# Attention with projections on one core: a new start, earlier loads of the second output weight, and a hand-ordered end

## The chip, the cores and the metric

The program runs on one core of one Trainium2 chip. The metric is the time of one execution in device microseconds (us), median of several. Runs carry a state, fast or slow: a run is called slow when it is over 1.5% longer than the fastest run of the same kernel. The ratios below compare fast runs alone; the medians are those with the few slow runs in them. Single runs of one kernel differ by 1 to 4 us here (the old kernel: 295.6 to 300.5 us in fast runs), so differences under about 1.5 us (0.5%) between two kernels are not read as results on their own.

## The reference

There are two independent problems, A and B, with equal shapes. The results stand side by side in the output.

```python
B, Sq, D = 8, 64, 448;  Hq, Hkv, Sk, Dh = 16, 8, 512, 256
q = (x @ wq).reshape(B, Sq, Hq, Dh)              # wq: 448 x 4096
k, v = k_cache, v_cache                          # each used by two query heads
p = softmax(q @ k.T * Dh**-0.5)
y = (p @ v).reshape(B, Sq, Hq*Dh) @ wo           # wo: 4096 x 448
out = concatenate([A_y, B_y], axis=-1)           # all bfloat16
```

K and V of both problems are 67 MB and are read once. wq and wo are 3.67 MB each for each problem.

## The kernel before

The work is cut into 128 units (64 for A, then 64 for B): one KV head of one batch, with its two query heads of 64 rows each as 128 rows. The program is planned in Python: every engine gets a fixed list of instructions, and waits on semaphores are put in where one engine needs another's result. TensorE (PE) does, for each unit, the transpose of K (every second unit; the other units' K is transposed by the DMA on its way in), the score matmuls, the transpose of P and the P·V matmuls. In between it does the query projection (wq) and the output projection (wo).

The loop runs over iterations `it`; in each one the stages of several units are at work:

```python
for it in range(it0, NU + D1 + 3):
    issue_dmas(it)               # loads needed up to iteration it + LEAD (5)
    ... pt_op(it - 3)            # transpose P of unit it-3
    ... qproj_chunk(...)         # query projection, up to two chunks
    ... qk_op(it); max_op(it)    # scores of unit it
    ... kt_op(it + 4)            # transpose K of unit it+4
    if it < NU - 1:              # output projection, as much as the level allows
        lvl = o_level(it)
        while o_fifo:
            if o_fifo[0][0] == 1 and o_fifo[0][1] == 3 and o_fifo[0][2] < n_tail + 0:
                break            # TAIL_GROUPS = 6 groups are kept for the end
            ...
            do_o_group(it)
    else:
        ...                      # the groups kept back, two per iteration
    ... pv_op(it - 3)
```

`o_level` spreads the output projection so that the planned TensorE time is level over the iterations that are left. All loads are issued by SyncE, in one order. K has three buffers of each kind and V has four (for two units each), so a load can be issued only when the buffer's last reader is done.

wo has one buffer for both problems, so each of B's eight wo loads (448 KB each) must wait for A's last use:

```python
def dma_wo(prob, g):
    plan.add("sp", lambda e: e.dma_start(wo_sb[:, g], src),
             writes=[("wo_sb", g)], ...)
def do_o_group(it):
    last = oproj_op(prob, bp, g)
    if prob == 0:
        if o_count[(0, bp)] >= 1 and bp == 3:
            dma_wo(1, g)         # SyncE waits here for TensorE
```

One more detail matters. An instruction can carry one wait; when an operation has several, the planner puts the others on earlier instructions of the same engine, up to 24 back ("hoisting"). So the wait for the first wq load stands on the last transpose of x, which does not need wq.

## Time and profile before

| | before |
|---|---|
| time, first four runs | 297.53 us median (296.32 to 297.9) |
| span of the profiled run | 295.8 us |
| TensorE busy | 281.9 us, 95% |
| first projection matmul / first score matmul | 8.1 / 18.9 us |
| TensorE waits for DMA after 20 us | 3.8 us |

From the page of the old kernel: the span, busy time and instructions by engine, and the 40 slices of TensorE's busy share and of its granted clock (in tenths).

```profile
span 295.8 us, 7089 instructions
...
PE 281.9 (95%) x2833; PEld 193.2 (65%) x2878; DVE 194.7 (66%) x519; ACT 177.2 (60%) x458; POOL 87.8 (30%) x132
...
PE   6899999999999999999999999999997799999995
...
PEclk9799999999999999999999999999999999999999
```

TensorE's waits for DMA after 20 us (what waited and for which load, then us in total, times, longest):

```profile
PE bank L631 <- DMA V_sb<-in_B_v_cache_dram: 1.6, 3, 1.0
PE bank L501 <- DMA K_sb<-in_B_k_cache_dram: 1.4, 2, 0.7
PE bank L566 <- DMA KTD_sb<-in_B_k_cache_dram: 0.8, 1, 0.8
```

TensorE is full except at the start, in slices 31 and 32, and at the very end. The timeline of TensorE at the start (start, length, line, operation, count, and in brackets the idle time before it and what ended it) shows why the first slices are poor:

```profile
1.41 3.38 PE L379 MATMUL bank<-ident 128*128 128x128 bf16 x30 [1.41 <-POOL ident L736]
4.80 1.04 PE L395 MATMUL bank<-ident,x_sb 128*112 128x128 bf16 x15
6.54 0.26 PE L395 MATMUL bank<-ident,x_sb 128*112 128x128 bf16 x1 [0.69 <-DMA wq_sb<-in_A_wq_dram]
8.12 5.27 PE L431 MATMUL bank<-xT_sb,wq_sb 112*128 112x512 bf16 x16 [1.32 <-ACT xT_sb L418]
...
15.27 3.62 PE L431 MATMUL bank<-xT_sb,wq_sb 112*128 112x512 bf16 x16
18.95 0.38 PE L501 MATMUL bank<-KT_sb,QT_sb 128*128 128x512 bf16 x1
```

L379 are warm-up matmuls, L395 the transposes of x, L431 the query projection, L460 transposes of K, L501 the scores. Fifteen transposes run at 4.80; the sixteenth stands until 6.54 for the wq load, and the projection until 8.12 for ScalarE's eviction. Its 16 matmuls then take 5.27 us; the next 16, at 15.27, take 3.62. Busy time by stretches (start:end, length, then busy time and count of PE, PEld, DVE, ACT, POOL, then granted clock, DMA share, GB/s):

```profile
8.00:20.00 12.00, 11.71 (x63) 5.41 (x65) 2.33 (x6) 5.43 (x10) 0.00 (x0) 0.86 0.91 245
100.00:140.00 40.00, 39.40 (x418) 27.70 (x424) 30.22 (x82) 26.31 (x71) 14.19 (x21) 1.00 1.15 300
220.00:240.00 20.00, 15.82 (x164) 10.31 (x164) 11.60 (x31) 8.86 (x25) 5.22 (x8) 1.00 1.14 318
```

The clock is 0.86 in the first of these stretches, and from 220 to 240 us TensorE is busy 15.8 of 20 us. The chain of waits there (start, length, what):

```profile
216.51 0.45 PE bank L501 x2
216.96 0.36 SPq L349
...
217.36 1.96 SPq L357
...
219.36 1.86 SPq L371
...
221.27 1.22 SPq L349
...
222.53 5.95 DMA K_sb<-in_B_k_cache_dram
...
228.53 0.39 PE bank L501
```

The chain leaves TensorE for SyncE's queue (SPq): the wo load (L349), a DMA transpose of K (L357), a V load (L371), another wo load, then a K load that lands 5.95 us after its issue. I read this chain as a queue held up by the wo loads' wait for TensorE.

### The profile page before, as it was taken

How to read it: one execution, taken by the hardware profiler on the slowest of the kernel's cores; microseconds unless marked ns; L12 is line 12 of the kernel's file. 1: busy time of each engine (PE TensorE's matmuls, PEld its weight loads, DVE VectorE, ACT ScalarE, POOL GpSimd, SP SyncE). 2: the span in 40 equal slices, each digit the busy share in tenths (PEclk: the TensorE clock that was granted, in tenths of full speed). 3: DMA queues.
4: the chain of work that ended last, by engine and by line, in shares of the span. 5: the costliest groups of instructions: out<-in, count | busy, mean ns of one | idle time of the engine just before them, and what ended most of it. 6: DMA issues, size and time to landing. Idle time of an engine off the chain costs nothing.

```text
span 295.8 us, 7089 instructions
## 1 busy us (share of the span) xinstructions
PE 281.9 (95%) x2833; PEld 193.2 (65%) x2878; DVE 194.7 (66%) x519; ACT 177.2 (60%) x458; POOL 87.8 (30%) x132
## 2 busy tenths in 40 slices
PE   6899999999999999999999999999997799999995
PEld 5345665776667677676766677777765467777663
DVE  1125544777687687777666668888875577777751
ACT  2467677565666666675777776665654446555551
POOL 0002221233233233333323323434422223333310
PEclk9799999999999999999999999999999999999999
DMA  7999999999999999999999999999999999999700
GB/s 207 245 249 293 356 276 338 289 369 293 278 364 291 239 358 264 278 295 345 284 273 307 320 290 304 258 331 321 289 368 300 363 295 287 294 293 289 245 18 16
DMA packets 112321, 84.09 MB, mean 284 GB/s; under 512 B 70304, under 2 KB 87712, under 8 KB 112288
## 3 DMA queue, kind: packets, MB, share of 16 engines
q1 hardware_dynamic: 112288, 83.64, 105.7%
q8 instruction: 22, 0.36, 0.5%
q14 instruction: 11, 0.09, 0.1%
HBM read 65.93 MB, written 0.92 MB: 226 GB/s over the span
## 4 chain that ended last, share of the span: by engine, by line
PE 82%; DMA 6%; ACT 5%; DVE 3%; SPq 2%; issue 1%
PE bank L590 17%; PE bank L501 16%; PE bank L431 16%; PE bank L631 15%; PE bank L460 10%; PE bank L566 8%; ACT P_sb L529 3%; DMA V_sb<-in_B_v_cache_dram 2%; DMA K_sb<-in_B_k_cache_dram 2%; DMA wq_sb<-in_A_wq_dram 2%; ACT OT_sb L609 2%; DVE negmax L520 2%; DVE KT_sb L479 1%; SPq L357 1%; SPq L371 1%
## 5 line engine op out<-in xcount | busy, mean ns | idle before, releaser
L546 POOL TENSOR_SCALAR P_sb<-P_sb,rinv 128x512 bf16<-128x512 bf16 x126 | 87.1, 692 | 195.7 <-DVE rinv L538 195.7
L520 DVE TENSOR_REDUCE negmax<-bank 128x1 f32<-128x512 f32 x128 | 88.5, 691 | 40.6 <-PE bank L501 40.2
L609 ACT ACTIVATE OT_sb<-bank 128x256 bf16<-128x256 f32 x128 | 49.0, 383 | 87.4 <-PE bank L590 87.4
L529 ACT ACTIVATE P_sb<-bank,negmax 128x512 bf16<-128x512 f32 x128 | 87.4, 683 | 0.2 <-DVE negmax L520 0.2
L575 DVE COPY PT_sb<-bank 128x512 bf16<-128x512 bf16 x128 | 54.2, 424 | 41.7 <-PE bank L566 40.2
L590 PE MATMUL bank<-PT_sb,V_sb 128*128 128x128 bf16 x1024 | 78.1, 219 | 0.0
L590 PEld LDWEIGHTS bank<-PT_sb,V_sb 128*128 128x128 bf16 x1024 | 66.0, 98 | 17.1 <-DVE PT_sb L575 0.3
L431 PE MATMUL bank<-xT_sb,wq_sb 112*128 112x512 bf16 x256 | 66.3, 387 | 1.3 <-ACT xT_sb L418 1.3
L631 PE MATMUL bank<-wo_sb,OT_sb 128*128 128x448 bf16 x256 | 59.3, 353 | 2.2 <-DMA V_sb<-in_B_v_cache_dram 1.6
L479 DVE COPY KT_sb<-bank 128x512 bf16<-128x512 bf16 x128 | 51.9, 406 | 8.3 <-PE bank L460 8.2
L566 PE MATMUL bank<-ident,P_sb 128*128 128x128 bf16 x512 | 50.0, 219 | 0.9 <-DMA KTD_sb<-in_B_k_cache_dram 0.8
L443 ACT ACTIVATE QT_sb<-bank 128x512 bf16<-128x512 f32 x64 | 38.2, 597 | 17.7 <-PE bank L431 16.5
L460 PEld LDWEIGHTS bank<-ident,K_sb 128*128 128x128 bf16 x512 | 33.2, 98 | 17.7 <-DVE KT_sb L479 4.6
L631 PEld LDWEIGHTS bank<-wo_sb,OT_sb 128*128 128x128 bf16 x256 | 23.8, 98 | 26.1 <-DMA V_sb<-in_B_v_cache_dram 4.0
L460 PE MATMUL bank<-ident,K_sb 128*128 128x128 bf16 x512 | 39.1, 219 | 0.6
L431 PEld LDWEIGHTS bank<-xT_sb,wq_sb 112*128 112x128 bf16 x256 | 22.9, 99 | 21.7 <-issue 2.2
L501 PE MATMUL bank<-KT_sb,QT_sb 128*128 128x512 bf16 x108 | 34.1, 379 | 2.5 <-DMA K_sb<-in_B_k_cache_dram 1.4
L566 PEld LDWEIGHTS bank<-ident,P_sb 128*128 128x128 bf16 x512 | 35.1, 105 | 1.6 <-DMA KTD_sb<-in_B_k_cache_dram 1.4
L501 PE MATMUL bank<-KTD_sb,QT_sb 128*128 128x512 bf16 x103 | 32.7, 379 | 1.4
L529 ACT ACTIVATION_READ_ACCUMULATOR P_sb<-bank,negmax 128x1 f32 x128 | 25.9, 202 | 0.0
L538 DVE RECIPROCAL rinv<-rowsum 128x1 f32<-128x1 f32 x128 | 19.6, 153 | 0.4 <-ACT P_sb L529 0.4
L501 PEld LDWEIGHTS bank<-KT_sb,QT_sb 128*128 128x128 bf16 x128 | 10.9, 98 | 7.6 <-DMA K_sb<-in_B_k_cache_dram 1.8
(18 smaller groups left out, 32.3 us busy)
## 6 DMA issues: line engine op xcount, KB each, us to landing
V_sb<-in_A_v_cache_dram SPq DMA_DIRECT2D x32, 512.0 KB, 6.4
V_sb<-in_B_v_cache_dram SPq DMA_DIRECT2D x32, 512.0 KB, 5.9
K_sb<-in_A_k_cache_dram SPq DMA_DIRECT2D x32, 256.0 KB, 6.5
K_sb<-in_B_k_cache_dram SPq DMA_DIRECT2D x32, 256.0 KB, 5.9
wq_sb<-in_A_wq_dram SPq DMA_DIRECT2D x8, 448.0 KB, 7.0
wo_sb<-in_A_wo_dram SPq DMA_DIRECT2D x8, 448.0 KB, 6.8
wq_sb<-in_B_wq_dram SPq DMA_DIRECT2D x8, 448.0 KB, 7.2
wo_sb<-in_B_wo_dram SPq DMA_DIRECT2D x8, 448.0 KB, 6.2
```

The costliest lines, as they stand in the source:

```text
L431: return e.matmul(banks[bk][:, 0:512], wq_sb[:, g, dtile, c0:c0 + 128], xT_sb[:, prob, dtile, :], start=(dtile == 0), stop=(dtile == 3))
L460: return e.transpose(bank[:, c:c + 128], K_sb[:, slot, kt, dt * 128:(dt + 1) * 128], ident[:, :])
L479: plan.add("dve", lambda e: e.tensor_copy(dst, bank[:, half * 512:(half + 1) * 512]), reads=[("bank", bk)], writes=[("KT_sb", ks, half)], ...
L501: return e.matmul(bank[:, 0:512], QT_sb[:, qs, b, dt, :], kt_t[:, ks, dt, :], start=(dt == 0), stop=(dt == 1))
L520: plan.add("dve", lambda e: e.tensor_reduce(negmax[:, s:s + 1], bank[:, 0:512], axis=AX.X, op=ALU.max, negate=True), reads=[("bank", bk)], ...
L529: plan.add("act", lambda e: e.activation(P_sb[:, u % NP, :], bank[:, 0:512], ACTF.Exp, bias=negmax[:, s:s + 1], scale=1.0, accum_out=rowsu ...
L546: plan.add("pool", lambda e: e.tensor_scalar(p, p, rinv[:, s:s + 1], 1.0, op0=ALU.mult, op1=ALU.mult), reads=[("rinv", s), ("P_sb", u % NP ...
L566: return e.transpose(banks_bf[PTB][:, kt * 128:(kt + 1) * 128], src, ident[:, :])
L575: plan.add("dve", lambda e: e.tensor_copy(dst, banks_bf[PTB][:, 0:512]), reads=[("bank", PTB)], writes=[("PT_sb", u % NPT)], name="ptev%d" ...
L590: return e.matmul(banks[OTB][:, dt * 128:(dt + 1) * 128], V_sb[:, slot, bl, kt, dt * 128:(dt + 1) * 128], PT_sb[:, u % NPT, kt, :], start= ...
L609: plan.add("act", lambda e: e.activation(dst, src, ACTF.Copy), reads=[("bank", OTB)], writes=[("OT_sb", ob, g, bl)], name="otev%d" % u)
L631: return e.matmul(banks[POB][:, 0:448], OT_sb[:, ob, 2 * g + hl, dt, :], wo_sb[:, g, hl * 2 + dt, :], start=first, stop=last)
```

## The change

The change has three parts, and its stated intent is to restructure the start and the end, to load wo early, and to keep wq in a ring of buffers.

```diff
 # 1. start: transposes of x in four groups without hoisted waits, four evictions,
 #    the first projection chunk waits tile by tile
-        xT_ops(0, bks=(PQB, POB), split=True)
-        sbanks = (OTB, PTB, PQB, POB)
+        xT_start((PQB, POB, OTB, PTB))          # no_hoist=True
+        sbanks = (SBK[0], PQB, POB, OTB)
...
-                qproj_chunk(0, 0, hl, dt, bk=sbanks[ci])
+                qproj_chunk(0, 0, hl, dt, bk=sbanks[ci], split=(ci == 0))
 # 2. memory: wq in a ring of four, one x and one xT, wo for both problems
-        wq_sb = sb("wq_sb", [112, 8, 4, 512], BF)
+        wq_sb = sb("wq_sb", [112, NWQ, 4, 512], BF)       # NWQ=4
-        wo_sb = sb("wo_sb", [128, 8, 4, 448], BF)
+        wo_sb = sb("wo_sb", [128, 2, 8, 4, 448], BF)
+    WO1_ITERS=(20, 56),
+            dma_reqs.append((w_lo + (g * (w_hi - w_lo)) // 7 + LEAD, 3, g, lambda g=g: dma_wo(1, g)))
-            if prob == 0:
-                if o_count[(0, bp)] >= 1 and bp == 3:
-                    dma_wo(1, g)
 # 3. end: two groups kept back instead of six, the last units written out by hand
-    TAIL_GROUPS=6,
+    TAIL_GROUPS=2,
-            if (prob, bp) != (1, 3):
-                o_total[0] -= 1
+            o_total[0] -= 1
...
+        pt_op(L - 2)
+        exp_op(L)
... (22 more lines that order the last three units by hand)
```

## The prediction

> **What bounds the kernel.** TensorE: 281.9 of the 295.8 us span (page, part 1), 82% of the chain that ended last (part 4). From 20 to 220 us it is busy 98 to 99% (busy time by stretches), in an order fixed when the program is built. So only TensorE's idle or slow time can be won back. I count four pieces.
>
> 1. Start-up wait. The timeline shows 15 of 16 transposes of x done by 5.84 us; the 16th stands until 6.54 because the wait for the first wq load (landed 6.50) was put on it. ScalarE then evicts two halves (0.61 us each); the first projection starts at 8.12.
> 2. Slow clock. The first eight projection matmuls (8.12 to 11.5) start 0.43 us apart, later ones 0.216: 1.7 us lost. Granted clock from 8 to 20 us: 0.86, or 3.4 us at half. The Trainium skill, "TensorE: Matmul & The Clock Gate", Part 1, says that an idle window of about 3.4 us halves the clock; this trace agrees in size (TensorE busy only 1.3 us between 4.8 and 8.1).
> 3. A stall from 220 to 240 us: TensorE busy 15.8 of 20, 4.2 us lost. The chain of waits goes there from the wo load through SyncE's issue queue to K and V loads. Each B wo load waits until TensorE is through with the A group in the same buffer, and all behind it in SyncE's queue waits too. SyncE's own waiting, its slack, falls from about 24 us in 40 to 4.2 us in 30 between 199 and 229, while the eight B wo loads go out; K and V then arrive late.
> 4. Tail: from the last score matmul (283.8) to the last output projection (292.95) TensorE idles only about 0.65 us. Then 0.62 us eviction and an output DMA of about 2 us.
>
> **What the change does.**
> - Transposes of x in four groups without early waits; evictions of about 0.44 us (DVE) and 0.61 us (ACT); the first projection chunk waits tile by tile. It can start when wq lands, about 6.6 us: **-1.5 us**. TensorE is then busy about 2.5 us of the same 3.4 us window, so I think (65%) the half clock does not come: **-1.1 us** expected.
> - B's wo gets its own memory (paid for by a four-slot wq ring and single x and xT), loaded over iterations 20 to 56 (about 60 to 135 us) without waiting on TensorE. The stall goes: **-4.1 us**. Cost: 3.67 MB over about 70 us, an estimate of 50 GB/s on top of about 305; the trace held 374 GB/s for 5 us without a stall, and SyncE has over 20 us of slack in each 40. **+0.5 us**.
> - Ring, x and xT reuse: a slot's readers finish two iterations before its load: **0**.
> - Tail: groups move ahead of or into the flush; the work is the same, and I estimate 0.6 to 0.8 us idle in the new dependency chain too: **0 us**.
>
> Sum -6.2: about **291 us**, range 288.8 to 293.8. Faster by over 2%: 0.55; within 2%: 0.43; slower: 0.02.
>
> **What would show each step.** First projection at about 6.6 us with 0.216 us spacing; TensorE over 98% busy between 220 and 240, no waits for K or V; less work after the last score matmul but no less idle; 60 to 135 us still over 98% busy at about 350 GB/s.
>
> **What would make it wrong.** The half clock returning at the start (+1.7); DMA saturating at iterations 20 to 56, moving the stall forward (up to +3); start-up loads not keeping up with the earlier TensorE; the tail saving more, if my chain is too long.

## The result, and the profile after

The new kernel takes 292.78 us median (292.31 to 294.32, 11 runs; a twelfth run, 295.60 us, these figures leave out); the old one in the same rounds took 297.53 (16 runs). The ratio is 0.9852, interval 0.9826 to 0.9877. Ratios here are the mean time of one kernel's fast runs over that of the other's fast runs of the same rounds, so not quite the ratio of the medians quoted. That is inside the predicted range; the prediction had given "faster by over 2%" the larger chance, 0.55.

The page of the new kernel:

```profile
span 290.7 us, 7089 instructions
...
PE 279.3 (96%) x2833; PEld 192.8 (66%) x2878; DVE 195.2 (67%) x521; ACT 176.2 (61%) x456; POOL 87.8 (30%) x132
...
PE   7999999999999999979999999999999999999995
...
PEclk9999999999999999999999999999999999999999
```

The dip at slices 31 and 32 is gone, and there is a new one at slice 18 (124 to 131 us by the slice length). TensorE at the start, where L401 are the transposes of x, L469 the projection and L547 the scores:

```profile
4.81 1.10 PE L401 MATMUL bank<-ident,x_sb 128*112 128x128 bf16 x16
6.49 3.61 PE L469 MATMUL bank<-xT_sb,wq_sb 112*128 112x512 bf16 x16 [0.57 <-DVE xT_sb L413]
...
15.66 0.38 PE L547 MATMUL bank<-KT_sb,QT_sb 128*128 128x512 bf16 x1
```

The first projection starts at 6.49 instead of 8.12 and the 16 matmuls take 3.61 us instead of 5.27. The first score matmul comes at 15.66 instead of 18.95: 3.29 us won. Busy time by stretches:

```profile
8.00:20.00 12.00, 11.83 (x73) 5.77 (x73) 3.81 (x9) 7.13 (x14) 0.46 (x1) 1.00 1.22 292
100.00:140.00 40.00, 36.88 (x389) 25.44 (x394) 27.95 (x77) 23.90 (x65) 13.14 (x20) 1.00 1.13 315
220.00:240.00 20.00, 19.84 (x214) 14.40 (x216) 15.77 (x42) 11.55 (x33) 6.92 (x10) 1.00 1.14 308
```

From 220 to 240 us TensorE is now busy 19.84 us. But from 100 to 140 us it is busy 36.88 of 40, where the old kernel had 39.40. The chain there:

```profile
116.89 0.24 PE bank L613 x4
117.13 0.10 SPq L368
...
117.28 0.84 SPq L382
...
118.16 8.40 DMA wq_sb<-in_B_wq_dram
...
126.61 1.05 PE bank L469 x4
```

It has the same form as in the old kernel: SyncE's queue, then a load that lands late, here a wq load of B. TensorE's waits for DMA after 20 us:

```profile
PE bank L469 <- DMA wq_sb<-in_B_wq_dram: 2.0, 2, 1.8
PE bank L469 <- DMA V_sb<-in_A_v_cache_dram: 0.8, 2, 0.5
```

They sum to 2.8 us, against 3.8 in the old kernel. So of the 4.1 us that I had expected from the wo part, 1.0 came.

At the end of the kernel, the time from the last unit's score weights to the end of the span fell from 12.66 to 9.24 us, by 3.42. But in the old kernel eight output projection groups stand in this stretch and in the new one three, and TensorE's busy time in it fell by as much, from 9.29 to 5.88 us. So nothing is won there net: five groups' work has moved forward.

### The profile page after: what moved, and what is told of

Read it like the earlier page. It is cut to its first block, busy times and chain, and to the rows that moved or that the text cites. A ratio compares the mean times of both kernels' runs of the same rounds, so it can differ in the third digit from the quotient of the medians.

```text
span 290.7 us, 7089 instructions
## 1 busy us (share of the span) xinstructions
PE 279.3 (96%) x2833; PEld 192.8 (66%) x2878; DVE 195.2 (67%) x521; ACT 176.2 (61%) x456; POOL 87.8 (30%) x132
## 2 busy tenths in 40 slices
DMA packets 112321, 84.09 MB, mean 289 GB/s; under 512 B 70304, under 2 KB 87712, under 8 KB 112288
## 4 chain that ended last, share of the span: by engine, by line
PE 80%; DMA 9%; ACT 4%; DVE 4%; issue 1%; SPq 1%
PE bank L639 17%; PE bank L685 16%; PE bank L547 16%; PE bank L469 14%; PE bank L506 9%; PE bank L613 8%; DMA wq_sb<-in_B_wq_dram 6%; ACT P_sb L575 3%; DMA V_sb<-in_A_v_cache_dram 2%; DVE negmax L566 1%; ACT OT_sb L659 1%; DMA x_sb<-in_A_x_dram 1%; DVE KT_sb L525 1%; SPq L382 0%; DVE xT_sb L413 0%
## 5 line engine op out<-in xcount | busy, mean ns | idle before, releaser
L469 PE MATMUL bank<-xT_sb,wq_sb 112*128 112x512 bf16 x256 | 65.0, 379 | 3.4 <-DMA wq_sb<-in_B_wq_dram 2.0
L489 ACT ACTIVATE QT_sb<-bank 128x512 bf16<-128x512 f32 x64 | 38.2, 597 | 19.5 <-PE bank L469 18.5
L613 PE MATMUL bank<-ident,P_sb 128*128 128x128 bf16 x512 | 49.4, 219 | 0.2 <-DVE P_sb L597 0.2
L469 PEld LDWEIGHTS bank<-xT_sb,wq_sb 112*128 112x128 bf16 x256 | 22.2, 97 | 23.4 <-DMA wq_sb<-in_B_wq_dram 2.4
L547 PE MATMUL bank<-KT_sb,QT_sb 128*128 128x512 bf16 x108 | 33.8, 379 | 1.1
L547 PE MATMUL bank<-KTD_sb,QT_sb 128*128 128x512 bf16 x103 | 32.7, 379 | 1.4
L547 PEld LDWEIGHTS bank<-KT_sb,QT_sb 128*128 128x128 bf16 x128 | 10.9, 98 | 5.7 <-DMA K_sb<-in_A_k_cache_dram 0.2
```

The source lines that it names most:

```text
L469: return e.matmul(banks[bk][:, 0:512], wq_sb[:, wslot, dtile, c0:c0 + 128], xT_sb[:, 0, dtile, :], start=(dtile == 0), stop=(dtile == 3))
L547: return e.matmul(bank[:, 0:512], QT_sb[:, qs, b, dt, :], kt_t[:, ks, dt, :], start=(dt == 0), stop=(dt == 1))
L613: return e.transpose(banks_bf[bk][:, kt * 128:(kt + 1) * 128], src, ident[:, :])
```

## The experiments

The k-th load in SyncE's order is a known load of the program, and the k-th weight load of TensorE a known matmul, so each load gets an issue time, a landing time, the time when its buffer's last reader was done, and the time of its first use. "Margin" below is first use minus landing.

All experiments but e4 and e8 start from the new kernel. Waits are TensorE's waits for DMA after 20 us, from the view of waits; slightly incomplete traces (2833 matmuls beside 2878 weight loads) make them good to some tenths.

| run | what | median us | ratio to old | waits, us |
|---|---|---|---|---|
| old | | 297.5 | 1 | 3.8 |
| new | | 292.8 | 0.9852 | 2.8 |
| e1 | wo of B at iterations 64 to 92 | 293.2 | 0.9857 | 3.2 |
| e2 | wq of B four iterations earlier | 295.5 | 0.9922 | 4.3 |
| e3 | wo of B in its old place, no wait | 296.1 | 0.9956 | 5.1 |
| e4 | old kernel, dummy matmuls at the start | 298.1 | 1.0010 | 4.8 |
| e5 | wo of B spread by hand | 293.7 | 0.9852 | 2.6 |
| e6 | deeper K buffers | 294.4 | 0.9875 | 3.7 |
| e7 | wo of B cut to 1/16 of its bytes | 289.4 | 0.9707 | 0.5 |
| e8 | old kernel with the new start | 296.3 | 0.9938 | 4.0 |
| e9 | pacing 5% higher | 291.6 | 0.9811 | (slow trace) |
| e10 | pacing 8% higher, wo spread | 290.2 | 0.9760 | 0.6 |
| e11 | new kernel with the old end | 297.8 | 1.0026 | 6.5 |
| e12 | start held for wq | 294.7 | 0.9908 | 2.4 |

Each interval is about ±0.005 (the new kernel's ±0.0025). e7's results are wrong on purpose; the others are correct.

### First four: where the wo loads stand, and the clock

e1:

```diff
-    WO1_ITERS=(20, 56),
+    WO1_ITERS=(64, 92),
```

> The changed kernel, with B's wo loads moved from iterations 20 to 56 to iterations 64 to 92, where no B wq load is under way. Theory (the new stall near 120 to 134 us comes from wo and wq loads competing in the same stretch): the stall of about 2.5 us goes, TensorE is over 98% busy from 100 to 140 us, no new stall at 140 to 200 us over 0.7 us, ratio to before about 0.977 (2.5 us under the changed kernel). Rival (the four-slot wq ring or the position of the wq loads alone is at fault): the wait for B's wq stays within 0.5 us, ratio about 0.985.

The stall at 100 to 140 us went as expected, and one of 3.2 us came at 180 to 220 us. The time did not change. So the place of the stall follows the place of the wo loads, which speaks against the ring of wq (no wq load of B has a wait in the program either), but "competition with wq" was not the cause: there is no wq load near e1's stall.

e2:

```diff
-            dma_reqs.append((q_iter(1, g, 0), 0, g, lambda g=g: dma_wq(1, g)))
+            dma_reqs.append((q_iter(1, g, 0) - (4 if g else 0), 0, g, lambda g=g: dma_wq(1, g)))
```

> The changed kernel, wo loads where it has them, but B's wq groups 1 to 7 requested four iterations earlier. If only the lead of the wq load was too short, the 1.8 us wait for wq goes, the waits for V (0.8 us) stay, ratio about 0.979. If the SyncE queue and the DMA engines are simply full in this stretch, the wait moves to K or V loads and at least 1.5 us of the 2.5 stay, ratio 0.983 or more.

The wait for wq went, and waits for V and K came in its place, 4.3 us in all. The second expectation held: the whole stream of loads is late here, not one load.

e3:

```diff
-            dma_reqs.append((w_lo + (g * (w_hi - w_lo)) // 7 + LEAD, 3, g, lambda g=g: dma_wo(1, g)))
...
+            if prob == 0 and bp == 3:
+                dma_wo(1, g)
```

> The changed kernel, but B's wo loads issued at the place in SyncE's queue where the old kernel issued them (after the output projection groups of A's last batch pair), into their own memory, so without waiting for TensorE. Theory of my prediction (the old stall at 220 to 240 us came from the wait for TensorE that blocked SyncE's queue): the stall shrinks below 1 us, and the new stall at 120 us is gone too, ratio about 0.977. Rival (eight wo loads within 28 us are too dense, wait or no wait): at least 3 us of the old 4.2 us stall stays, ratio about 0.988 (the 2.5 us gone, 3 to 4 us back).

The loads go to their own memory, so they have nothing to wait for. This tests the mechanism that the prediction named for the old stall. Busy time by stretches in e3:

```profile
120.00:140.00 20.00, 19.64 (x209) 13.78 (x212) 15.11 (x41) 12.70 (x34) 6.92 (x10) 1.00 1.16 290
200.00:220.00 20.00, 16.61 (x181) 11.44 (x185) 13.13 (x37) 9.73 (x28) 6.23 (x9) 1.00 1.13 336
220.00:240.00 20.00, 18.52 (x201) 13.20 (x202) 14.44 (x39) 10.11 (x30) 6.46 (x10) 1.00 1.16 310
```

The stall at 120 to 140 us is gone, and 4.9 us are lost from 200 to 240 us, without any wait of the wo loads for TensorE. So such a stall does not need that wait. What e3 and the old kernel share is eight loads of 448 KB within about 14 iterations. The ratio, 0.9956, is even above the rival's 0.988.

The old kernel's own trace says the same. Setting each wo load of B beside the one group of TensorE that it waits for in the program's plan, only the second of the eight waited, 0.4 us at most; the others were issued when SyncE came to them, the last at 227.52 us, about 8 us after its group's weight loads (219.56). The prediction's mechanism fell.

e4:

```diff
+                if last:
+                    plan.add("pe", last, reads=[("x_sb", prob), "ident", ("wq_sb", 0)],
...
         xT_ops(0, bks=(PQB, POB), split=True)
+        warm_op(22)
```

(The first lines keep the last transpose waiting for wq.)

> The old kernel, with 22 dummy matmuls in the wait between the last transpose of x (still held until the first wq lands) and the first projection, which so starts at about 8.1 us as before. Theory (TensorE's idle time before it brings the half clock): the first eight projection matmuls start 0.216 us apart, not 0.43, the first score matmul comes 1.7 us earlier (about 17.3 us), ratio about 0.9943. Rival (the first 3.4 us of dense wide matmuls run at half clock whatever went before): spacing stays 0.43, ratio 1.000.

In the profiled run the projection ran at full speed (16 matmuls in 3.63 us). But in four of the six runs the granted clock was 0.994, so the fill did not prevent the slow stretch, and the time did not fall. The one trace proves nothing for the fill, since the old kernel without it also has runs at full clock (two of its eight fast runs of this set). Nor did the fill close every gap: the last transpose waited 0.90 us for wq before it. More on this under e12.

### The loads as a stream

The landing times explain the first three. In all traces looked at, the loads (outputs apart) land in the order of their issue, 226 of 226, and when they are behind, one lands directly after the other: the median distance is 0.68 us for a K load, 0.88 for a DMA-transposed K, 1.44 for a V load of two units, 1.25 for wo and 1.5 for wq (new kernel). Two iterations need 0.68 + 0.88 + 1.44 = 3.0 us of this, so one iteration needs 1.5 us. In the new kernel an iteration lasts 2.16 us between units 10 and 40, and 1.78 between units 80 and 100. What is left is 0.3 to 0.7 us per iteration, and these medians leave out the longer distances (up to 3.5 us). A wo load takes 1.25 of it. Eight of them in 14 iterations of 1.78 us: (1.5 + 8·1.25/14 − 1.78)·14 = 6 us short, an estimate; the margin at 180 to 200 us in the old kernel was 4.4 us in the median. The estimate would leave a stall of 1.6 us; the waits were 3.8, so it gets the direction and not the size.

The margin shows it directly. Median margins of the loads used in a stretch: new kernel 2.8 us at 80 to 100 us, 1.5 at 100 to 120, 0.7 at 120 to 140 (smallest 0.04); old kernel 2.8, 3.4 and 2.5 there, and 0.25 at 220 to 240.

It also shows where the prediction misread SyncE. The view of waits had SyncE waiting for TensorE during some 24 of 40 us, and I took that for slack. (TensorE signals all its work on one counting semaphore, and the view takes the counter's latest step for the end of a wait, though the value waited for may have been reached long before.) SyncE and TensorE's scores in the new kernel, in order of time:

```profile
119.84 0.60 PE L547 MATMUL bank<-KTD_sb,QT_sb 128*128 128x512 bf16 x2
...
120.22 1.70 SPq L368 DMA_TRANSPOSE KTD_sb<-in_A_k_cache_dram  x1
...
123.24 0.43 SPq L359 DMA_DIRECT2D wo_sb<-in_B_wo_dram  x1
...
123.72 4.04 SPq L368 DMA_TRANSPOSE KTD_sb<-in_A_k_cache_dram  x1
```

The transpose issued at 123.72 takes 4.04 us. It loads into a buffer whose last reader, the score matmul of unit 45, is the first line, over at about 120.4. It waited for nothing that TensorE did. In the new kernel 51 of 61 such issues with a known buffer came over 1 us after the buffer was free, and they still took 1.2 to 4.2 us (median 2.1), where the least is 1.22. Setting every issue beside the group that it waits for in the program's plan, SyncE waited for TensorE about 1 us in all from 20 to 140 us in the old kernel, and its issues filled 36 to 39 of each 40 us. So the slack was not there. That the DMA stream held the issues back is the likely reading, but not shown by itself: in e7 below, which hardly stalls, 30 of the 61 came late, with a median of 1.6 us and up to 4.0, and issues filled 36 of the 40 us from 100 to 140.

### Second four: bytes, depth, and the start alone

e5 (same kernel, the eight wo loads at hand-picked iterations):

```diff
+    WO1_AT=(16, 26, 37, 48, 68, 75, 82, 89),
-            dma_reqs.append((w_lo + (g * (w_hi - w_lo)) // 7 + LEAD, ...
+            dma_reqs.append((CFG["WO1_AT"][g] + LEAD, ...
```

> The changed kernel with B's wo loads issued at iterations 16, 26, 37, 48, 68, 75, 82, 89: about 7 to 11 iterations apart, none between 50 and 67 where four wq loads go out. New theory: loads land one behind the other, K and V take 1.5 us of landing time per iteration of about 1.9 us, so only some 0.4 us per iteration is left; a wo load takes 1.25 us of it, a wq load 1.5, and what exceeds it eats the 3 to 5 us by which K and V land ahead of their use. Then this spacing fits, the waits for DMA sum to under 0.7 us (2.8 in the changed kernel, 4 in the old) and the time falls by about 2 us under the changed kernel, ratio about 0.978. Rival (what stalls is chance, or any place costs the same 2.5 us): ratio 0.985.

The rival held: 2.6 us of waits, now in four places (60 to 80, 120 to 140, 180 to 200, 200 to 220 us), ratio 0.9852.

e6:

```diff
-    LEAD=5,
+    LEAD=6,
```

> The changed kernel with loads asked for six iterations ahead instead of five, and with that four K buffers instead of three of each kind (V unchanged). If the look-ahead is the buffer that the wo and wq loads eat, one iteration (1.9 us) more of it cuts the stalls from 2.5 to 1.5 us or less, ratio about 0.981. If the rate is the limit for long enough, or V is what comes late, less than 0.7 us is won, ratio 0.984 or more.

Nothing was won (0.9875, waits 3.7 us). One more K buffer of each kind does not help while V keeps its four, or while the shortage lasts longer than one iteration; the run does not tell these two apart.

e7:

```diff
+            dst = wo_sb[:, prob, g]
+            if prob == 1:
+                src, dst = src[0:8], wo_sb[0:8, prob, g]
...
+        plan.add("pool", lambda e: e.memset(wo_sb[:, 1].rearrange("p g j n -> p (g j n)"), 0.0),
```

> Wrong results on purpose: the changed kernel with each of B's wo loads cut to 8 of 128 partitions (28 KB instead of 448), the rest of that memory zeroed at the start; the eight issues stay in SyncE's queue where they were. If the bytes are what costs, the stall at 100 to 140 us goes (under 0.5 us) and the ratio falls to about 0.977. If the places in SyncE's queue cost, at least 1.5 us of stall stay, ratio about 0.983.

The clearest answer. All waits for DMA that are left after 20 us:

```profile
PE bank L550 <- DMA K_sb<-in_A_k_cache_dram: 0.5, 1, 0.5
```

The issues stand in the queue as before; the bytes are gone, and with them the stall: 289.35 us, ratio 0.9707. So it is the transfers that cost, not the places in the queue. (Fewer bytes also means fewer DMA packets, 108417 against 112321 in all; the run does not tell these two apart.) B's 3.67 MB of wo cost the new kernel about 1.45% (0.9852 against 0.9707), and about as much where e1 and e5 put them; e3's dense place costs about 2.5%.

e8 is the old kernel with part 1 of the diff alone.

> The old kernel with the new start alone (grouped transposes of x, four evictions, first projection chunk waiting tile by tile). By my sum: first score matmul 3.3 us earlier than in the old kernel's trace (15.2 instead of 18.5 us), granted clock 1.00, and the stall at 220 to 240 us stays near 4 us: ratio about 0.989. Rival (the loads limit the whole, so an earlier start is waited away later): the stall there grows by over 1.5 us, ratio 0.994 or more.

The ratio is 0.9938, between the two expectations. The first score weights load at 15.5 instead of 18.5 us (3.0 won) in the traces, and the later stall:

```profile
200.00:220.00 20.00, 18.61 (x206) 13.39 (x209) 15.71 (x43) 10.98 (x31) 7.62 (x11) 1.00 1.13 338
220.00:240.00 20.00, 16.86 (x176) 11.25 (x177) 11.96 (x32) 8.43 (x24) 5.02 (x9) 1.00 1.16 317
```

3.1 us are lost from 220 to 240 us and 1.4 from 200 to 220, together 4.5; the old kernel lost 4.2 and 0.2 there. So the start is not waited away. Why the time shows 1.8 us and not 3.3 is seen in the single runs: the old kernel has a granted clock below 0.995 in 15 of its 28 fast runs of the three sets, and those are longer than its other fast runs by 2.2, 1.7 and 1.5 us. The profiled run of the old kernel was one of them (0.993). Kernels with the new start (the new kernel, e1 to e3, e5 to e11) show it in 1 of 71 runs. So the slow stretch costs about 1.8 us in about half of the runs, 1.0 on average, and not 1.7 in all.

### Last four: pacing, the end, the start

e9:

```diff
-    O_LEVEL=1.0,
+    O_LEVEL=1.05,
```

> The changed kernel with one number changed: the pacing level of the output projection raised by 5%, so that TensorE does more of it in the iterations where it is at hand and less later. Nothing is loaded earlier or later in the order. If loads and TensorE run at nearly equal rates and the loads need time, longer iterations up to the 56th give it to them: the first score matmul of unit 40 comes 1 to 3 us later than in the changed kernel, the DMA waits at 100 to 160 us shrink by at least 1.2 us, ratio about 0.979. Rival (the place of the wo loads alone matters): waits stay at 2.5 us, ratio 0.985.

The profile of e9 fell in a run at a granted clock of 0.657 (420 us; one run of the old kernel in this set did the same, 423 us), so its trace cannot be set beside the others. The five fast runs give 0.9811, with all but one between 290.9 and 291.7 us: in the direction of the theory, and short of the 0.979 expected. But the interval, 0.9765 to 0.9858, holds the rival's 0.985 too, so e9 does not decide. The trace half of the expectation stays unread.

e10:

```diff
-    O_LEVEL=1.0,
+    O_LEVEL=1.08,
+    WO1_AT=(24, 29, 35, 40, 46, 67, 77, 87),
... (the line of e5 that reads WO1_AT)
```

> Pacing raised by 8% and B's wo loads issued at iterations 24, 29, 35, 40, 46, 67, 77, 87, away from the four close wq loads. An attempt at a better version. If both help, DMA waits of TensorE after 20 us sum to under 0.8 us and the ratio is about 0.975, near the 0.971 of the run without the bytes. If pacing only moves the shortage to iterations 64 to 100, the waits stay above 2 us, ratio 0.983 or more.

This version beats both kernels: 290.16 us (289.23 to 290.88), ratio 0.976, interval 0.972 to 0.9801. All waits for DMA after 20 us:

```profile
PE bank L470 <- DMA V_sb<-in_A_v_cache_dram: 0.6, 1, 0.6
```

The iterations between units 40 and 64 last 2.14 us here and those between 64 and 80 last 2.12, where e7, which does not wait, has 2.04 and 1.98; the later ones (100 to 127) are shorter, 1.79 against 1.95. TensorE does the same work, earlier, while the loads catch up. Spreading alone (e5, at other places) gave nothing and pacing alone (e9) about 0.4% by its ratio, which is within the noise. That both are needed is not shown, since e9 and e10 differ in the level too.

e11 is the new kernel with part 3 of the diff taken back (`TAIL_GROUPS=6`, the old loop, no hand-ordered end).

> The changed kernel with the old tail and its pacing: six groups kept back for the end instead of two, the old loop after the last iteration. My prediction gave the tail 0 us, which holds for the end of the kernel: from the last score matmul of the last unit to the end, idle time of TensorE within 0.3 us of the changed kernel's. New theory: the groups kept back make iterations 10 to 40 about 2.9 us shorter (62.0 against 64.9 us between the score matmuls of units 10 and 40), which the loads lack, so the DMA waits at 100 to 160 us grow from 2.5 to 4 us or more, ratio about 0.991. Rival (the tail is neutral): ratio 0.985.

The new kernel loses everything: 297.79 us, ratio 1.0026. Its waits for DMA after 20 us:

```profile
PE bank L469 <- DMA V_sb<-in_A_v_cache_dram: 3.3, 4, 1.1
PE bank L469 <- DMA wq_sb<-in_B_wq_dram: 1.7, 2, 1.3
PE bank L685 <- DMA V_sb<-in_A_v_cache_dram: 1.5, 3, 0.7
```

They sum to 6.5 us against 2.8. The prediction's 0 us for the end itself was right: the end takes 12.66 us from the last unit's score weights in e11 and 9.24 in the new kernel, and the five groups that moved account for the difference. But work moved to where wo is loaded. Between units 10 and 40 the old plan takes 62.0 us (old kernel) and the new one 64.9, both without a stall of note. Those 2.9 us are time for two wo loads. Of the 5.2 us between the two traces' spans (295.9 and 290.7), 3.7 are waits for DMA in this view; about 1.5 are not assigned.

e12:

```diff
-                plan.add("pe", emits, reads=[("x_sb", 0), "ident"], writes=[("bank", bk)],
+                plan.add("pe", emits, reads=[("x_sb", 0), "ident", ("wq_sb", 0)], writes=[("bank", bk)],
```

> The changed kernel with all transposes of x held until the first wq load has landed (about 6.4 us), so TensorE idles from 4.7 to 6.4 us and the first projection starts at about 7.9 instead of 6.5 us. If idle time at the start brings the half clock, granted clocks of 0.992 to 0.995 come back in at least two of the six runs, as in about half of the old kernel's runs, and those runs are about 2 us longer than the others. If not, all stay at 0.999 or 1.0 and the time rises by 1.5 us at most, ratio 0.990.

One run of six had 0.994, so the first expectation failed. The time rose by 1.7 us (0.9908 against 0.9852), which is the second's 1.5 within the noise; only its "all stay at 0.999 or 1.0" failed, in that one run. The trace still shows a slow start that the mean clock hides. TensorE at the start of e12, and its busy time by stretches with the granted clock:

```profile
6.32 1.95 PE L401 MATMUL bank<-ident,x_sb 128*112 128x128 bf16 x16 [1.53 <-DMA wq_sb<-in_A_wq_dram]
8.07 4.42 PE L469 MATMUL bank<-xT_sb,wq_sb 112*128 112x512 bf16 x16
```

```profile
0.00:8.00 8.00, 5.06 (x46) 4.80 (x47) 0.97 (x3) 1.28 (x1) 0.68 (x6) 1.00 0.77 210
8.00:20.00 12.00, 11.89 (x71) 5.63 (x70) 3.03 (x7) 6.19 (x11) 0.00 (x0) 1.00 1.15 272
```

The 16 transposes take 1.95 us, where the new kernel needs 1.10, and their weights load 0.107 us apart instead of 0.056; the first projections are 0.39 to 0.46 us apart until 9.7 us. By this spacing TensorE ran at half speed, while the granted clock says 1.00. In the trace's records the first grant of the full clock comes at 9.69 us; the mean counts what lies before the first record as full. In the other traces that first grant falls anywhere from 4.3 to 7.0 us. In the old kernel's trace it comes at 4.66, is withdrawn at 8.07 and given back at 11.48: 3.41 us each time.

These figures allow one more step. In the 12 traces that can be used (e3's has no clock records, e9's is the slow run), the time from the first grant to each later change is a whole multiple of 3.41 us (83 to 85 of them up to the end of the kernel). So I cut each trace into windows of 3.41 us, counted from its first grant. In 13 windows at full clock TensorE was busy for 1.44 us or less, and after each the clock was withdrawn: 12 of them at the end of a kernel, the other the old kernel's 4.66 to 8.07 (1.44 us). All other windows at full clock, with 1.64 us or more, kept it, those of the stalls included. In the new kernel the window of 4.40 to 7.82 has 2.70. Where the windows fall differs from trace to trace. An estimate: if windows could fall anywhere with equal chance, the old start as profiled would have one under 1.55 us in about 40% of the runs and the new start in none, beside 15 of 28 and 1 of 71 measured. So too little work in one window fits both. It does not explain e4, whose profiled start would never go under 1.9 us and which still has 0.994 in four of six runs; and no run set out to test the limit.

## Why the prediction was right, and where it was wrong

The time (292.78 us) lies in the range, and the difference from the old kernel is 4.4 us by the ratio, where 6.2 were expected. That the sum came out so near is partly luck: the part about wo fell short, and the pacing that came with the new end, which the prediction gave nothing for, made up for it. With the old end (e11, 297.79 us) the same start and the same wo loads would have missed the range.

- Start, −1.5 us: right. First projection at 6.49 instead of 8.12 us in the traces.
- Half clock, −1.1 us: about right in size (1.0 on average), but not as argued. I had put a 65% chance on removing a loss of 1.7 us that I took to occur always. It occurs in about half of the old kernel's fast runs (15 of 28), and the new start removes it almost always (1 of 71). Too little work in one window of 3.41 us fits the traces as its cause, but e4 does not fit.
- The stall, "−4.1 us" with "+0.5 us" of cost: the step that failed. Of 3.8 us of waits for DMA, 2.8 are left. Two parts of the argument were wrong. The wait for TensorE in SyncE's queue was not what made the old stall (e3: without it, 5.1 us of waits; in the old trace itself, 0.4 us of such waiting at most). And "SyncE has over 20 us of slack in each 40" was no slack: from 20 to 140 us it waited for TensorE about 1 us, and its issues filled 112 of the 120. The cost of the loads at iterations 20 to 56 was mis-sized: 2.5 to 2.8 us in place of 0.5. The check "374 GB/s for 5 us without a stall" was too short a stretch: over 20 us in which TensorE lost more than 2 us, the traces hold 296 to 339 GB/s (120 to 140 us in e6 296, 220 to 240 in the old kernel 318 and in e4 339). The rate alone does not tell a shortage, though: e10 moved 336 GB/s from 200 to 220 us without a stall. The prediction had named this outcome among what would make it wrong ("moving the stall forward (up to +3)"), and its check "60 to 135 us still over 98% busy" failed: 36.88 of 40 us, 92%, from 100 to 140.
- The end, "0 us": right for the end of the kernel (nothing net) and wrong for the change. With the old end the new kernel is as slow as the old kernel (e11). By the ratios of e8, e11 and the new kernel, the start brings 0.6%, the wo part (with the ring) costs 0.9%, and the end with its pacing brings 1.7%. These three come from different sets of runs, each good to ±0.5%, so the sizes are rough; the waits for DMA in the traces (4.0, 6.5, 2.8 us) have the same order.
- Ring of wq, single x and xT, 0 us: nothing speaks against it. No wq load of B waits for its buffer in the program's plan.

Of the page figures, the Trainium skill's "DMA: Bandwidth & Descriptors" (Specifications) gives an HBM limit of about 358 GB/s per core; this kernel's mix stayed under it over every 20 us looked at (339 at most), though single slices of 7 us reach 369, and ran short of loads at 296 to 339. Whether that limit is what binds here, no run shows.

## What to carry to other kernels

When a load moves, set its landing time beside the length of the iterations that it moves to, and ask how far ahead the other loads land there; if TensorE's time per iteration and the loads' are nearly equal, every byte costs its time. What got it back here was a change in the length of the iterations (moving TensorE's work to where loads are dense). A queue engine that "waits" in the profile may not be idle: look up whether the buffer it is said to wait for had long been free. A part of a change that is neutral where it stands can still be the one that pays, by what it moves elsewhere; take parts back one by one before crediting them.

## What the Trainium skill lacked or had wrong

- "TensorE: Matmul & The Clock Gate", Part 1, gives the idle window of about 3.4 us that halves the clock. The trace agrees on the length (withdrawn and given back 3.41 us apart), but the page gives no activity level that keeps the clock. Here TensorE was not idle in the window that lost it, but busy for 1.44 of 3.41 us; windows with 1.64 us or more kept it.
- None of the pages says that a mean granted clock can hide a slow start: e12 has 1.00 from 0 to 8 us while its transposes load 0.107 us apart, against 0.056 at full speed.
- "DMA: Bandwidth & Descriptors", Queues, rings and completion order, says that completion is not first-in first-out per issuing engine. That is a statement of what is guaranteed; here all 226 loads landed in the order of issue in each of the eight traces checked. The page has no figure for a mix of plain and transposing loads; this one ran short at 296 to 339 GB/s.
- "Perfetto Trace Analysis", Optimizing DMA Performance, takes solid DMA slices of the issuing engine as a sign that descriptor generation is the limit. In the new kernel the transposes' issues stretched from 1.22 to up to 4.2 us, and e7 shows that the number of issues was not the limit: with the issues left in place and 15/16 of wo's bytes taken away, the waits for DMA fell from 2.8 to 0.5 us, while SyncE's issues still filled 36 of the 40 us from 100 to 140.
